# Gated mix of a state space layer and an MLP on one core: two spreading copies moved on VectorE, a group of TensorE transposes moved by one matmul and copied out in halves

## The chip, the cores and the metric

The kernel runs on one core of a Trainium2 chip. The metric is the device time of one execution in microseconds; the median of three executions is compared. The engines are called PE (TensorE matmul; PEld is its weight load), DVE (VectorE), ACT (ScalarE), POOL (GpSimd) and SP (SyncE, which only issues DMAs here).

## The reference, cut to what matters

```python
x = A_x                                              # 2048 rows of 448, bfloat16
g = sigmoid((x * gate_w).sum(-1, keepdims=True))
# a: Bu = x @ B_bar.T;  h[t] = Lam_bar * h[t-1] + Bu[t] (complex);  a = 2 Re(h @ C.T) + x * Dskip
# b: silu(x @ w1) @ w2                               # 448 -> 1792 -> 448
return g * a + (1 - g) * b
```

## The kernel before, in words

The 2048 rows of `x` are read as 1024 pairs, so that every pair has an even and an odd row of 448 columns. `XT` holds `x` transposed, with its columns on the 128 partitions: blocks 0 to 3 for the even rows, 4 to 7 for the odd ones. The 448 columns are three full blocks of 128 (`j` = 0, 1, 2) and a rest of 64 (`j` = 3). Block 3 is filled with the columns 384 to 511 of a pair, so the last 64 columns of the even row lie in its lower 64 partitions. `XR` holds that rest a second time in the other 64 partitions: matmuls of 64 rows can then run in both halves of the PE array at once. The rows are worked in four parts of 512: even 0, even 1, odd 0, odd 1.

There is no scheduler. A `Tracker` writes one list of instructions per engine in the order of the program text. Before each operation it adds the waits that the named buffers ask for: a reader waits for the last writer of a name, and a writer waits for the last writer and for all readers since then. Each of the eight PSUM banks is one such name (`ps0` to `ps7`), whatever part of the bank is used. Engines run their lists strictly in order.

**The front, up to about 10 us.** Part even 0 doesn't come by a transposing DMA. It is loaded as rows into `XH` (the start of `XN`) in six DMAs, `XA0` to `XA3` for the columns 0 to 255 and `XB0`, `XB1` for the columns 256 to 383 and 384 to 511. PE transposes 128x128 squares of it into PSUM (`turn_k`, line 493), and DVE copies them into `XT` (`turned_k` line 503 for one square, `turned_x` line 509 for two or four). `turn_x(j, i)` issues the two squares `2i` and `2i+1` of block `j`. All of them go to bank 6 for `j` = 0 and 2 and to bank 7 for `j` = 1 and 3 unless another is given.

`ffn1_first` is a generator that runs the first six column blocks of `x @ w1` for part even 0 in six banks, and stops at fixed places so that the transposes can be put between (line 435). For `j` = 0 its matmuls cover 128 or 256 columns; for `j` = 1 and 2 there are six matmuls each over all 512 columns, numbered `n` = 0 to 5. The order of PE's list in the front is: three matmuls of `j` = 1, four small matmuls that turn parameter rows into columns (`mm_cols`, line 474), four transposes for block 2, the other three matmuls of `j` = 1, four transposes for block 3, six matmuls of `j` = 2, and then three pairs with the rest (`ffn1_rem`, line 449). From there on `lanes` (line 362) carries the rest of `x @ w1` and of the state space input, and ACT applies silu (line 457).

**DVE's list from 10 to 27 us** prepares tables of sines and cosines. `phases(pt)` (lines 614 and 616) is two operations over 128x1024 float32, on POOL for `pt` = 0 and 3 and on DVE for 2 and 1; `phases2(pt)` (line 621) is a DVE operation with two inputs that needs the result of `phases(pt)`. In between lie: two copies that spread the rows `gate_w` and `Dskip` from 32 to 64 and from 64 to 128 partitions of `GD` (line 672, 896 bfloat16 a partition); `decays` (four operations on 128x4); `swap_xr("dve", 1, 0)` (line 241), which fills `XR` for the last columns of part even 1; and copies in `BT` and `BR` (lines 680 and 682). `GD` is read by `gate` (654) and `skip` (662), which come behind `phases2(1)`. Line 901 is the first step of the scan and reads what PE has put in PSUM; the first one follows the `XR` copies of the odd rows (line 238).

Of the kernel before, what the change touches and what calls it, by code (L numbers as in the profile page):

```python
# [150 lines left out]
def gated_mix(nc, A_x, A_Lambda_re, A_Lambda_im, A_B_re, A_B_im, A_C_re, A_C_im, A_log_dt,  # L151
              A_Dskip, B_x, B_w1, B_w2, gate_w, out):
    with ExitStack() as ctx:
# [75 lines left out]
            return T.dma("sp", lambda e: e.dma_start_transpose(dst, src), reads=reads,  # L229
                         writes=[key, *also], group=group)  # L230

        XE = [(["XTe000", "XTe001", "XTe010", "XTe011", "XTe02"], ["XTe03"]), (["XTe1"], ["XTer1"])]
        XO = [([f"XTo{h}"], [f"XTr{h}"]) for h in range(2)]

        def swap_xr(eng, h, odd):
            hs = slice(h * 512, (h + 1) * 512)
            if odd:
                T.op(eng, lambda e: e.tensor_copy(XR[0:64, hs], XT[64:128, 7, hs]), reads=XO[h][1],
                     writes=[f"XR{h}b"])
            else:  # L240
                T.op(eng, lambda e: e.tensor_copy(XR[64:128, hs], XT[0:64, 3, hs]), reads=XE[h][1],
                     writes=[f"XR{h}a"])
# [93 lines left out]
        def nxt():  # L336
            n_bank[0] += 1
            return BANKS[(n_bank[0] - 1) % len(BANKS)]
# [7 lines left out]
        def rem_keys(odd, h, p):  # L346
            return (XO if odd else XE)[h][1] if (p is UP) == bool(odd) else [f"XR{h}{'b' if odd else 'a'}"]

# [48 lines left out]
        def ff(fb):  # L397
            i, c = fb // 2, fb % 2
            return i + 3 * c if i < 3 else i + 3 + 2 * c if i < 5 else i + 5 + 2 * c

        def wj(fb):
            i, c = fb // 2, fb % 2
            return [f"W1Ej0{c}", "W1Ej1", "W1Ej2"] if i < 3 else ["W1Ed0", "W1Ed2"] if i < 5 else ["W1Ee0", "W1Ee1"]

        def w1(fb):
            return lambda p, j: W1E[p, j, ff(fb) * 128:(ff(fb) + 1) * 128] if j < 3 else \
                W1E[p, j, fb // 2 * 128:(fb // 2 + 1) * 128]

        def rem_ffn1(odd, h, fb):
            return [*[f"W1E{'r' if fb < 6 else 's'}{c}" for c in range(2)], *rem_keys(odd, h, LO), *rem_keys(odd, h, UP)]  # L410
# [6 lines left out]
        def ffn1_pair(c, fb, p=None):  # L417
            odd, h = c // 2, c % 2
            banks = at(p) if p is not None else [nxt(), nxt()]
            return (*[(banks[i], odd, h, w1(fb + i)) for i in range(2)],  # L420
                    wj(fb) + wj(fb + 1) + (XO if odd else XE)[h][0], rem_ffn1(odd, h, fb),
                    lambda: ffn1_act(c, fb, banks[0], 2))

        def ffn1_first():
            banks = [nxt() for _ in range(NF1)]
            for fb in (0, 2, 4):
                T.op("pe", lambda pe, fb=fb, bank=banks[fb]: pe.matmul(
                    ps[:, bank, 0:128], W1E[:, 0, ff(fb) * 128:(ff(fb) + 1) * 128], XT[:, 0, 0:128],
                    start=True, stop=True), reads=["W1Ej00", "XTe000a"], writes=[f"ps{banks[fb]}"])
            for j, h in ((0, 0), (0, 1), (1, None), (2, None)):  # L430
                for n, fb in enumerate((0, 2, 4, 1, 3, 5)):
                    k = h == 0 and n < 3
                    c = slice(0, 512) if h is None else slice(128 if k else 256 * h, 256 * h + 256)
                    bank = banks[fb]
                    T.op("pe", lambda pe, fb=fb, bank=bank, j=j, h=h, c=c, k=k: pe.matmul(  # L435
                        ps[:, bank, c], W1E[:, j, ff(fb) * 128:(ff(fb) + 1) * 128], XT[:, j, c],
                        start=(h == 0 and not k), stop=(h == 0 and not k), skip_group_check=(h != 0 or k)),
                        reads=[f"W1Ej{j}" if j else f"W1Ej0{fb % 2}"] + (
                            ["XTe02"] if j == 2 else [f"XTe0{j}{h}"] if h is not None else [f"XTe0{j}0", f"XTe0{j}1"]),
                        writes=[f"ps{bank}"])  # L440
                    if (j, h, n) in ((0, 0, 2), (0, 0, 5), (1, None, 2), (1, None, 5)):
                        yield
            yield banks

# [10 lines left out]
        def ffn1_act(c, fb, bank, n=1):  # L455
            a = AT[c % 2]
            T.op("act", lambda e: e.activation(a[:, fb:fb + n, :], ps[:, bank:bank + n, :], AF.Silu),  # L457
                 reads=[f"ps{bank + i}" for i in range(n)], writes=[f"AT{c % 2}_{fb + i}" for i in range(n)])

        def ffn1(c, f0=0, ahead=None):  # L460
            for fb in range(f0, NFB, 2):
                pair(*ffn1_pair(c, fb), last=(c == 3 and fb == NFB - 2))
                if ahead and fb == 8:
                    ahead()
                yield
# [31 lines left out]
        def turn_x(j, i):  # L497
            for k in (2 * i, 2 * i + 1):
                turn_k(j, k)
# [6 lines left out]
        def turned_x(j, i=None, b=None):  # L506
            c, key = (slice(0, 512), f"XTe0{j}") if i is None else (slice(256 * i, 256 * i + 256), f"XTe0{j}{i}")
            b = PB[j] if b is None else b
            T.op("dve", lambda e: e.tensor_copy(XT[:, j, c], ps[:, b, 0:256].bitcast(BF16)[:, c]),
                 reads=[f"ps{b}"], writes=[key])  # L510
# [5 lines left out]
        turned_x(1, 0)  # L516
        warm(1, 4)
        first = ffn1_first()
        next(first)
        for k in (2, 3):  # L520
# [3 lines left out]
        for k in (2, 3):  # L524
# [5 lines left out]
        T.op("dve", lambda e: e.tensor_copy(  # L530
            PV[:, :, :], ps[:, 7, 256:288].rearrange("p (t c) -> p t c", c=8)[:, :, 0:4]),
            reads=["pv", "ps7"], writes=["PV"])
        for i in range(2):
            turn_x(2, i)
        turned_x(2)
        next(first)
        for i in range(2):
            turn_x(3, i)
# [12 lines left out]
        def c1(n, pt):  # L551
            i = pc(n)
            return P[:, i, pt:pt + 1]
# [33 lines left out]
        first = next(first)  # L587
# [6 lines left out]
        def decays():  # L594
            ptt("lr", col("mag"), col("cs"), ALU.mult, ["mag", "cs"])
            ptt("li", col("mag"), col("sn"), ALU.mult, ["mag", "sn"])
            pts("nli", col("li"), -1.0, None, ALU.mult, ALU.bypass, ["li"])
            T.op("dve", lambda e: e.tensor_tensor(c1("lis", 3), c1("li", 3), SG[:, 0:1], ALU.mult),
                 reads=["li"] + SGN, writes=["lis"])
# [6 lines left out]
        def phase(pt):  # L606
            if pt < 3:
                return FP[:, pt, :]
            return Q3[:, :, :].rearrange("p a b -> p (a b)").bitcast(F32)

        def phases(pt, eng="pool"):
            f2 = "f2s" if pt == 3 else "f2"
            X, RR = phase(pt), G[:, GP[pt], :]
            T.op(eng, lambda e: e.tensor_scalar(X, IOTA[:, :], c1(f2, pt), 0.0, ALU.mult, ALU.add),
                 reads=["IOTA", f2], writes=[f"F{pt}"])
            T.op(eng, lambda e: e.tensor_scalar(RR, X, 1.0, MAGIC, ALU.mult, ALU.add),
                 reads=[f"F{pt}"], writes=[f"G{GP[pt]}"])

        def phases2(pt):
            X, RR = phase(pt), G[:, GP[pt], :]  # L620
            T.op("dve", lambda e: e.scalar_tensor_tensor(X, RR, MAGIC, X, ALU.subtract, ALU.subtract),
                 reads=[f"F{pt}", f"G{GP[pt]}"], writes=[f"F{pt}"])
# [45 lines left out]

        phases(0)
        phases(2, "dve")  # L670
        for n in (32, 64):
            T.op("dve", lambda e, n=n: e.tensor_copy(GD[n:2 * n, :, :], GD[0:n, :, :]), reads=["GW", "DB"],
                 writes=["GW", "DB"])
        phases2(0)
        decays()
        swap_xr("dve", 1, 0)
        phases2(2)
        phases(3)
        phases(1, "dve")
# [168 lines left out]
        def bt(p, j, m):  # L848
            if m == 6:
                return BR[p, j, :]  # L850
            c = (m // 2) * 128 + D * (m % 2)
            return BT[p, j, c:c + 128]
# [3 lines left out]
        def bu_even(pt, h, p=None, q=None):  # L856
# [4 lines left out]
            def done():  # L861
# [5 lines left out]

            return (*[(b[i], 0, h, lambda p, j, i=i: bt(p, j, m + i)) for i in range(2)], BTK[0:2] + XE[h][0],
                    BTK + XE[h][0] + rem_keys(0, h, LO) + rem_keys(0, h, UP), done)

# [5 lines left out]
        def bu3_even(p, q):  # L876
            b = at(p)

            def done():
# [7 lines left out]

            return (*[(b[h], 0, h, lambda p, j: bt(p, j, 6)) for h in range(2)], ["BR"] + XE[0][0] + XE[1][0],
                    ["BR"] + rem_keys(0, 0, LO) + rem_keys(0, 1, UP), done)
# [278 lines left out]
        f = ffn1(2)  # L1168
# [70 lines left out]
def bass_gated_mix__ssm_conv_s5__dense_activation_silu__prompt_kernel(nc, *args):  # L1239
    gated_mix(nc, *args)  # L1240
# [28 lines left out]
```

## Time and profile before

| | |
|---|---|
| median of 3 runs | 136.72 us (136.68 to 136.97) |
| the profiled execution | 136.32 us, its span 134.8 us, granted PE clock 1.0 |
| busy in the span | PE 131.4 us (97%), DVE 115.5 (86%), ACT 93.7 (70%), POOL 15.9 (12%) |
| chain that ended last | PE 93%, DMA 3%, ACT's queue 1%, DVE 1% |
| DMA | 11.78 MB, mean 87 GB/s |

The span runs from the first to the last instruction; the rest of the execution's time lies around it. In a timeline a line gives the start in us from the start of the span, the duration, the engine, the line of the kernel, the operation, and in brackets the idle time before it with what ended it. Matmuls are pipelined: a 128x512 matmul is recorded with 0.38 us, but in a dense stream one starts every 0.216 us, and a 128x128 transpose every 0.055 us. A few matmul records are missing from a trace.

### The profile page before, as it was taken

How to read it: one execution, taken by the hardware profiler on the slowest of the kernel's cores; microseconds unless marked ns; L12 is line 12 of the kernel's file. 1: busy time of each engine (PE TensorE's matmuls, PEld its weight loads, DVE VectorE, ACT ScalarE, POOL GpSimd, SP SyncE). 2: the span in 40 equal slices, each digit the busy share in tenths (PEclk: the TensorE clock that was granted, in tenths of full speed). 3: DMA queues.
4: the chain of work that ended last, by engine and by line, in shares of the span. 5: the costliest groups of instructions: out<-in, count | busy, mean ns of one | idle time of the engine just before them, and what ended most of it. 6: DMA issues, size and time to landing. Idle time of an engine off the chain costs nothing.

```text
span 134.8 us, 2637 instructions
## 1 busy us (share of the span) xinstructions
PE 131.4 (97%) x1074; PEld 65.7 (49%) x1075; DVE 115.5 (86%) x154; ACT 93.7 (70%) x146; POOL 15.9 (12%) x32
## 2 busy tenths in 40 slices
PE   7899999999999999999999999999999999999993
PEld 7544444444444554444445544445555555555552
DVE  1379999917999798999999999999999999994554
ACT  0469698899939999769999597796124337879200
POOL 7109358550000000000000000000000000000000
DMA  3999959996994310000211000000000000222123
GB/s 103 258 284 191 181 129 220 179 379 182 264 188 98 71 46 0 0 0 5 66 45 45 5 0 0 0 5 0 0 0 0 0 0 15 92 94 76 68 81 124
DMA packets 25248, 11.78 MB, mean 87 GB/s; under 512 B 17619, under 2 KB 24726, under 8 KB 25238
## 3 DMA queue, kind: packets, MB, share of 16 engines
q1 hardware_dynamic: 23252, 10.47, 33.4%
q10 hardware_dynamic: 1986, 1.17, 3.0%
q8 instruction: 8, 0.13, 0.4%
q14 instruction: 2, 0.02, 0.0%
HBM read 5.34 MB, written 1.84 MB: 53 GB/s over the span
## 4 chain that ended last, share of the span: by engine, by line
PE 93%; DMA 3%; ACTq 1%; DVE 1%; issue 0%
PE ps L362 44%; PE ps L801 16%; PE ps L816 16%; PE ps L1054 15%; DMA XN<-in_A_x_dram 3%; PE ps L435 1%; ACTq L226 1%; DVE TMPS L1078 1%; PE ps L449 1%; PE ps L493 0%
## 5 line engine op out<-in xcount | busy, mean ns | idle before, releaser
L362 PE MATMUL ps<-XT,W1E 64*128 64x512 bf16 x325 | 41.4, 376 | 0.0
L457 ACT ACTIVATE AT<-ps 128x1024 bf16<-128x1024 f32 x28 | 28.2, 1019 | 7.4 <-PE ps L362 7.2
L362 PEld LDWEIGHTS ps<-XT,W1E 64*128 64x128 bf16 x325 | 16.9, 94 | 19.0 <-ACT AT L457 0.3
L362 PE MATMUL ps<-XT,BT 64*128 64x512 bf16 x156 | 22.4, 377 | 0.0
L816 PE MATMUL ps<-W,AT 64*128 64x448 bf16 x224 | 21.5, 349 | 0.0
L801 PE MATMUL ps<-W,AT 128*128 128x448 bf16 x112 | 21.4, 353 | 0.0
L816 PEld LDWEIGHTS ps<-W,AT 64*128 64x128 bf16 x224 | 10.9, 94 | 10.4
L801 PEld LDWEIGHTS ps<-W,AT 128*128 128x128 bf16 x112 | 10.9, 98 | 10.5 <-issue 0.4
L845 ACT ACTIVATE BT<-ps,GT 128x448 bf16<-128x448 f32 x8 | 5.1, 633 | 13.2 <-PE ps L801 13.2
L901 DVE SCALAR_TENSOR_TENSOR HS<-VE,P,ps 128x512 bf16<-128x512 bf16 (+1 forms) x13 | 9.6, 780 | 3.8 <-PE ps L362 3.8
L362 PEld LDWEIGHTS ps<-XT,BT 64*128 64x128 bf16 x156 | 8.1, 94 | 9.3 <-DVE HS L901 0.4
L945 DVE TENSOR_TENSOR_SCAN G<-P,Q 128x1024 f32<-128x1024 f32 (+1 forms) x6 | 11.4, 1922 | 0.0
L1054 PE MATMUL ps<-CO,VE 128*128 128x448 bf16 (+2 forms) x63 | 11.1, 332 | 0.0
L1054 PE MATMUL ps<-CO,HS 128*128 128x448 bf16 x56 | 11.1, 353 | 0.0
L362 PE MATMUL ps<-XR,W1E 64*128 64x512 bf16 x25 | 9.3, 376 | 0.0
L1054 PEld LDWEIGHTS ps<-CO,VE 128*128 128x128 bf16 x63 | 6.0, 98 | 4.8
L1054 PEld LDWEIGHTS ps<-CO,HS 128*128 128x128 bf16 x56 | 5.5, 98 | 5.1
L898 DVE TENSOR_TENSOR Q<-G,COS 128x2048 bf16<-128x2048 f32 (+1 forms) x4 | 7.0, 1756 | 0.1
L898 DVE TENSOR_TENSOR Q<-G,SIN 128x2048 bf16<-128x2048 f32 (+1 forms) x4 | 7.0, 1751 | 0.0
L863 ACT ACTIVATE VE<-ps 128x1024 bf16<-128x1024 f32 x6 | 6.1, 1019 | 1.2 <-PE ps L362 1.2
L865 ACT ACTIVATE ps<-VE,P 128x1024 f32<-128x1024 bf16 x6 | 6.7, 1118 | 0.2
L901 DVE SCALAR_TENSOR_TENSOR VE<-HS,P,FP 128x512 bf16<-128x512 bf16 (+1 forms) x7 | 6.6, 977 | 0.1
(126 smaller groups left out, 181.2 us busy)
## 6 DMA issues: line engine op xcount, KB each, us to landing
W<-in_B_w_dram SPq DMA_DIRECT2D x2, 784.0 KB, 5.9
XN<-in_A_x_dram SPq DMA_DIRECT2D x1, 896.0 KB, 5.3
out_dram<-OT SPq DMA_DIRECT2D x8, 112.0 KB, 1.7
out_dram<-TMPS SPq DMA_DIRECT2D x7, 112.0 KB, 1.7
HS<-HS SPq DMA_DIRECT2D x4, 128.0 KB, 2.3
XN<-in_A_x_dram SPq DMA_DIRECT2D x1, 384.0 KB, 3.8
W1E<-in_B_w_dram SPq DMA_DIRECT2D x1, 256.0 KB, 5.0
W1E<-in_B_w_dram ACTq DMA_DIRECT2D x1, 256.0 KB, 5.3
```

Source lines behind the costliest of these rows:

```text
L226: return T.dma(eng, lambda e: e.dma_start(dst, src), writes=[key], group=group)
L362: ins = pe.matmul(ps[:, bank, :], w(p, j), xh(odd, h, j, p), start=start and j == js[0], stop=stop and j == js[-1], skip_group_check=seeded)
L457: T.op("act", lambda e: e.activation(a[:, fb:fb + n, :], ps[:, bank:bank + n, :], AF.Silu), reads=[f"ps{bank + i}" for i in range(n)], wri ...
L801: ins = pe.matmul(ps[:, bank, 0:D], a[:, fb, q * 128:(q + 1) * 128], W2[:, ff(fb), :], start=(first and fb == 0), stop=(fb == NFB - 1), sk ...
L816: ins = pe.matmul(ps[:, bank, 0:D], a[p, fb, q * 128:(q + 1) * 128], W2[p, ff(fb), :], start=(start and fb == 0), stop=(not start and fb = ...
L845: T.op("act", lambda e: e.activation(bs(tile), ps[:, bank, 0:D], AF.Copy, scale=sc), reads=[f"ps{bank}", "GT2" if h else "GRI"], writes=ks)
L863: T.op("act", lambda e: e.activation(VE[:, m:m + 2, hs], ps[:, b[0]:b[0] + 2, :], AF.Copy), reads=[f"ps{i}" for i in b], writes=vs)
L865: T.op("act", lambda e: e.activation(ps[:, o[0]:o[0] + 2, :], VE[:, m:m + 2, hs], AF.Copy, scale=c1("lr", pt)), reads=vs + ["lr"], writes= ...
L898: T.op("dve", lambda e: e.tensor_tensor(o, a, b, op), reads=reads, writes=writes)
L901: T.op("dve", lambda e: e.scalar_tensor_tensor(o, a, s, b, ALU.mult, ALU.add), reads=reads, writes=writes)
L945: T.op("dve", lambda e: e.tensor_tensor_scan(G[:, c, w], rb, Q1[:, c, w], init, ALU.mult, ALU.add), reads=[f"Q1{c}", "rr", f"G{c}"], write ...
L1054: ins = pe.matmul(ps[:, bank, c], state(kt, odd, m), CO[:, m, c], start=False, stop=(m == YB[-1]), skip_group_check=True)
```

## The change

Two independent edits, both in the order of the text.

1. The transposes of block 2 move behind one more matmul of `j` = 1 (`n` = 3), for which `ffn1_first` gets one more stop. The copy of the block out of bank 6 is made in two halves of 256 columns, each right behind the two transposes that it reads. The name `XTe02` becomes `XTe020` and `XTe021`, and every reader takes both.
2. The two spreading copies of `GD` move behind `phases2(0)` and `swap_xr("dve", 1, 0)` in DVE's list.

```diff
-        XE = [([..., "XTe02"], ["XTe03"]), (["XTe1"], ["XTer1"])]
+        XE = [([..., "XTe020", "XTe021"], ["XTe03"]), (["XTe1"], ["XTer1"])]
...
-                            ["XTe02"] if j == 2 else ...
+                            ["XTe020", "XTe021"] if j == 2 else ...
...
-                    if (j, h, n) in ((0, 0, 2), (0, 0, 5), (1, None, 2), (1, None, 5)):
+                    if (j, h, n) in ((0, 0, 2), (0, 0, 5), (1, None, 2), (1, None, 3), (1, None, 5)):
                         yield
...
+        next(first)
         for i in range(2):
             turn_x(2, i)
-        turned_x(2)
+            turned_x(2, i)
         next(first)
...
         phases(0)
         phases(2, "dve")
+        phases2(0)
+        swap_xr("dve", 1, 0)
         for n in (32, 64):
             T.op("dve", lambda e, n=n: e.tensor_copy(GD[n:2 * n, :, :], GD[0:n, :, :]), reads=["GW", "DB"],
                  writes=["GW", "DB"])
-        phases2(0)
         decays()
-        swap_xr("dve", 1, 0)
         phases2(2)
```

The order of PE's list in the front is then: three matmuls of `j` = 1, `mm_cols`, the matmul `n` = 3, two transposes, two transposes, two matmuls of `j` = 1, four transposes for block 3, six matmuls of `j` = 2.

More of the change, by code (lines that the diff above doesn't have):

```diff
@@ L230, in ldt @@
                          writes=[key, *also], group=group)
-        XE = [(["XTe000", "XTe001", "XTe010", "XTe011", "XTe02"], ["XTe03"]), (["XTe1"], ["XTer1"])]
+        XE = [(["XTe000", "XTe001", "XTe010", "XTe011", "XTe020", "XTe021"], ["XTe03"]), (["XTe1"], ["XTer1"])]
         XO = [([f"XTo{h}"], [f"XTr{h}"]) for h in range(2)]
@@ L438, in ffn1_first @@
                         reads=[f"W1Ej{j}" if j else f"W1Ej0{fb % 2}"] + (
-                            ["XTe02"] if j == 2 else [f"XTe0{j}{h}"] if h is not None else [f"XTe0{j}0", f"XTe0{j}1"]),
+                            ["XTe020", "XTe021"] if j == 2 else [f"XTe0{j}{h}"] if h is not None else [f"XTe0{j}0", f"XTe0{j}1"]),
                         writes=[f"ps{bank}"])
-                    if (j, h, n) in ((0, 0, 2), (0, 0, 5), (1, None, 2), (1, None, 5)):
+                    if (j, h, n) in ((0, 0, 2), (0, 0, 5), (1, None, 2), (1, None, 3), (1, None, 5)):
                         yield
```

## The prediction

> **What bounds the kernel now.** I read the chain that ended last first, since it says which engine a microsecond has to be taken from. It is the following, in order of time (start, duration, what):
>
> ```profile
> 2.77 4.00 DMA XN<-in_A_x_dram
> 6.77 0.05 issue
> 6.82 0.40 PE ps L493 x4
> 7.21 0.05 issue
> 7.27 0.59 PE ps L435 x2
> 7.86 0.22 PE ps L493 x4
> 8.08 1.29 PE ps L435 x6
> 9.38 0.75 PE ps L449 x6
> 10.13 31.76 PE ps L362 x294
> ```
>
> From 6.77 us, when the DMA with columns 256 to 383 (XB0) lands, the chain is PE without a hole. The matmul records bear that out: with 0.216 us for 512 columns, start to start, the steps from 7.05 us to the last matmul leave only two holes, 0.096 us before line 449 and 0.092 us before line 801, both where PE changes between matmuls of 128 and of 64 rows. So a time that the front of PE's list gains or loses arrives at the end unchanged; what DVE, ACT and POOL gain arrives only if PE waits for it.
>
> Second, the timeline of the front, for the place of edit 1, and two rows of 5 us, which show the same kind of hand-over:
>
> ```profile
> 4.89 0.22 DVE L503 COPY XT<-ps 128x128 bf16<-128x128 bf16 x1
> ...
> 5.02 0.11 PEld L493 LDWEIGHTS ps<-ID,XN 128*128 128x128 bf16 x2 [0.15 <-DVE XT L503]
> ...
> 5.35 0.29 DVE L509 COPY XT<-ps 128x256 bf16<-128x256 bf16 x1 [0.25 <-PE ps L493]
> ...
> 6.47 0.24 PE L474 MATMUL ps<-ID,R 128*128 128x4 bf16 x4
> ...
> 6.81 0.23 PEld L493 LDWEIGHTS ps<-ID,XN 128*128 128x128 bf16 x4 [0.19 <-DMA XN<-in_A_x_dram]
> 6.82 0.40 PE L493 MATMUL ps<-ID,XN 128*128 128x128 bf16 x4
> ...
> 7.25 0.42 DVE L509 COPY XT<-ps 128x512 bf16<-128x512 bf16 x1 [0.32 <-PE ps L493]
> ```
>
> PE has a hole of 0.24 us in front of the transposes (the last of mm_cols starts at 6.55 and takes a step of 0.025) and waits there for XB0. The copy of the block starts 0.258 us after the last transpose started (6.994 to 7.252), as at 5 us (5.092 to 5.350).
>
> Third, the timeline of DVE and POOL for edit 2, and from the list of waits the first long wait of DVE behind it:
>
> ```profile
> 12.00 1.37 POOL L616 TENSOR_SCALAR G<-FP 128x1024 f32<-128x1024 f32 x1
> ...
> 12.49 2.40 DVE L672 COPY GD<-GD 32x896 bf16<-32x896 bf16 x2
> ...
> 13.53 1.12 POOL L614 TENSOR_SCALAR Q<-IOTA,P 128x1024 f32<-128x1024 f32 x1 [0.17 <-POOL G L616]
> ...
> 14.93 1.23 DVE L621 SCALAR_TENSOR_TENSOR FP<-G,FP 128x1024 f32<-128x1024 f32 x1
> ```
>
> ```profile
> DVE HS L901 <- PE ps L362: 3.8, 2, 3.2
> ```
>
> **Edit 1, the matmul that moves (gain).** Matmul n = 3 has nothing to wait for behind mm_cols: its weights and block 1 are those of n = 0 to 2. It starts at about 6.58 and its 0.216 us step ends at 6.80, so it lies whole in the 0.24 us hole. XB0 lands at 6.771 and its weight load can start at 6.81 as now, so the transposes keep their place: gain 0.216 us.
>
> **Edit 1, the halves (loss).** All four transposes write bank 6. The first half copy now stands between the second and the third of them and reads that bank, so the third transpose must wait for it: a wait that the order of the changed kernel shows on PE (line 493, on DVE) and that before doesn't have. In PE's list everything is queued behind it. Its price from rows: the second transpose starts at 6.882 as now; 0.258 us later the half copy can start, at 7.140 (DVE is free, its PV copy ends at 6.93); 128x256 takes 0.292 us (the row at 5.35); from the end of a DVE copy to the waiting transpose are 0.057 us (4.970 to 5.027, and 5.102 to 5.158 in the next wait). The third transpose starts at 6.882 + 0.258 + 0.292 + 0.057 = 7.489. In the stream it would have been 0.055 us behind the second, so the hole is 0.552 us. Nothing can fill it, for PE runs in order.
>
> **Sum for PE.** The fourth transpose starts at 7.554 (the step behind a wait is 0.065, as from 6.817 to 6.882), n = 4 and 5 at 7.609 and 7.825, the transposes of block 3 from 8.041, the first matmul of j = 2 at 8.265. Before it starts at 7.921: 0.34 us later, which is 0.552 - 0.216 and a slow step.
>
> **Can something else be later still?** The second half copy starts 0.258 us behind the fourth transpose, at 7.81, and ends at 8.10; the first matmul of j = 2 needs 0.06 us from there, 8.16, and comes at 8.265. XB1 landed at 7.476 and the weights of j = 2 at 7.681. On DVE two operations for the decay rates (0.15 and 0.16 us) wait behind both halves: they start at 8.02 in place of 7.59, 0.43 later, and ACT's exponential, its table load (1.28 us) and the two row DMAs of GD in ACT's queue with them (they landed at 11.44 and 11.66, and GD is now touched only behind 14.9). ACT is then free for the first silu at 10.00, and that silu, which starts at 9.74 now, comes with PE at 10.09. So 0.08 us of cover is left; without it PE would lose the excess through the banks. The copies of block 3 and of XR shift by the same 0.34 as PE.
>
> [...] The rows give 0.292 us for a half and 0.425 for the whole, so two halves cost 0.159 us more. [...]
>
> **Edit 2.** No instruction is added. The two GD copies took 1.11 and 1.26 us, although a copy of 64x896 in BT takes 0.39 (line 680). They end 0.24 us after the POOL operations beside them end (13.604 after 13.363, 14.895 after 14.652): they stood waiting for POOL. Once moved, phases2(0) must itself wait for POOL's line 616, which ends at 13.36; the GD copies covered that wait, and DVE now stands idle from 12.46 to about 13.42, some 0.95 us. Whether the operation then goes ahead of POOL's next one (start 13.53) the trace doesn't show. If it does, it ends at 14.65, and the XR copy (0.32 with its gap), two GD copies (0.42 each) and decays (0.52) follow: phases2(2) starts at 16.33 to 17.3, with none or one 0.95 us POOL operation in the way. If POOL goes first, phases2(0) is held to 14.65 and phases2(2) starts at 17.53. Before it starts at 16.91: -0.6 to +0.6 us. I take +0.2, since POOL's next operation will most likely fall on the XR copy. POOL's own later phases move as much.
>
> The nearest row for the two operations meeting is a POOL operation on 128x4 that takes 0.34 us by itself and 1.01 when it starts at 22.41 beside a line 621 that runs to 23.37. [...]
>
> On PE all of this costs nothing, at either end: the next reader of DVE's work is the matmul at 17.96, which needs the XR copy that ended at 16.88 and now ends earlier; the BT copy is read 2.0 us after it ends, the odd XR copies 2.9 and 4.4 us after. What is left of a delay ends in DVE's idle 3.2 us before line 901 at 30.55, which waits for PE. Without that cover the 0.6 us would come on top.
>
> **Rivals.** *The half copy doesn't hold PE* (faster). Then only the 0.216 us count, giving 136.50. This happens if the third transpose starts less than 0.27 us (0.216 + 0.055) after the second. Against it: the one copy alone takes 0.292, and the hand-over at 5.02 us shows PE standing for just such a copy.
>
> *The weights are late anyway* (little or no change). The weights of the next pairs landed at 9.557 us, and PE first needed them at 9.76: 0.2 us of room. The unprofiled runs were 0.4 us longer than the profiled one; if that is loads that land late, PE waits there before the change too, and up to all of the 0.34 is swallowed: 136.72 to 136.95. Against it: the profile shows no such wait.
>
> *The hole is bigger* (slower). If XB0 lands before 6.55, there was no hole to fill and the whole 0.55 counts: 137.27. The same sign has a silu that ACT starts late, beyond its 0.08 us.
>
> **How the numbers follow.** The profiled execution would take 136.32 + 0.34 = 136.66. The median stands 0.40 above it; the hole is a wait inside the chip and doesn't depend on that, so 136.72 + 0.34 = 137.06, 0.25% more. 0.2% of 136.72 is 0.27 us, about what a measurement of this kernel can tell from no change. Chances: my forecast 0.66, late weights 0.14, bigger hole 0.11, no hold 0.09. For the range I take late weights in full at its lower end and the bigger hole at its upper, with 0.10 us for the scatter of a median (the three runs lie 0.04 below to 0.25 above theirs): 136.62 to 137.37. Only no hold lies outside. Slower by over 0.2%: the bigger hole and 0.51 of the forecast's 0.66 (its 0.34 lies only 0.07 over the bound), 0.62. Within 0.2%: the other 0.15 and late weights, 0.29. Faster: 0.09.
>
> **What would show it.** In the profile after: no wait for XB0 of 0.19 us before line 493, but a hole of about 0.55 us between the second and the third transpose of block 2, ended by DVE line 509; two copies of 128x256 at about 7.14 and 7.81; the first matmul of j = 2 at 8.27; the span near 135.2; GD copies of about 0.4 us each, and DVE idle before line 621 near 13 us. I am wrong if the third transpose follows the second at once, if PE shows a new hole behind 8.3 us, or if the first matmul of j = 2 starts before 8.1.

## The result, and the profile after

The changed kernel takes 137.08 us (median of 22 runs, 136.39 to 137.78), the kernel before 136.72 (22 runs, 135.98 to 137.58). The ratio is 1.0031 with a 95% interval of 1.0016 to 1.0047: 0.42 us more, between 0.22 and 0.64. Two later comparisons of 12 runs, on two different chips, gave 1.0049 for edit 1 alone and 1.0050 for the full change. In the latter, one of the 12 runs, at 139.12 us, counts as slow and is left out. The forecast was 137.06, slower.

The profiled execution of the changed kernel took 136.39 us, the shortest of the 22, and its span is 134.8 us, the same as before. That alone would read as no change. The chain that ended last, in order of time, shows where the time is (start, duration, what):

```profile
3.68 0.33 PE ps L427 x3
...
6.27 0.08 PE ps L474 x4
...
6.43 0.29 PE ps L493 x2
6.72 0.02 issue
6.74 0.30 DVE XT L509
7.04 0.05 issue
7.09 0.29 PE ps L493 x2
7.37 0.43 PE ps L435 x2
7.80 0.22 PE ps L493 x4
8.03 1.29 PE ps L435 x6
```

A DVE copy has come into the chain, between two and two transposes, where there was none; behind the last line shown it is PE without a hole again, as before: from the first matmul of line 449 to the end of the span are 125.52 us in both profiles. So what differs between the two lies in the front. And the chain now goes back to the first matmuls instead of to XB0: in this execution XB0 landed at 6.01 us (before: 6.77), and the first weights of line 427 at 3.62 (before: 3.97), so PE's work began 0.35 us earlier. Counted from there, the first matmul of j = 2 comes 4.202 us after the first of line 427 (3.663 to 7.865), and 3.908 us before (4.013 to 7.921): 0.29 us more, although the execution of before had a wait of 0.24 us for XB0 in this stretch and the changed one has none. The earlier start of 0.35 us hides it in the span.

The timeline of the front shows the hold itself, with PE's idle time before the third transpose and what ended it in brackets:

```profile
6.43 0.27 PE L493 MATMUL ps<-ID,XN 128*128 128x128 bf16 x2
...
6.74 0.29 DVE L509 COPY XT<-ps 128x256 bf16<-128x256 bf16 x1 [0.17 <-PE ps L493]
7.08 0.11 PEld L493 LDWEIGHTS ps<-ID,XN 128*128 128x128 bf16 x2 [0.56 <-DVE XT L509]
7.09 0.29 PE L493 MATMUL ps<-ID,XN 128*128 128x128 bf16 x2 [0.39 <-DVE XT L509]
```

By the single records the second transpose starts at 6.484 and the third at 7.088. Less the step of 0.055 that is a hole of 0.549 us.

Edit 2, in the timeline of DVE and POOL and in the list of waits between 10 and 33 us:

```profile
11.94 1.37 POOL L617 TENSOR_SCALAR G<-FP 128x1024 f32<-128x1024 f32 x1
...
13.34 1.23 DVE L622 SCALAR_TENSOR_TENSOR FP<-G,FP 128x1024 f32<-128x1024 f32 x1 [0.93 <-POOL G L617]
...
13.47 2.08 POOL L615 TENSOR_SCALAR Q<-IOTA,P 128x1024 f32<-128x1024 f32 x1 [0.17 <-POOL G L617]
...
14.59 1.11 DVE L241 COPY XR<-XT 64x512 bf16<-64x512 bf16 x1
...
15.73 0.80 DVE L675 COPY GD<-GD 32x896 bf16<-32x896 bf16 x2
...
16.99 1.22 DVE L622 SCALAR_TENSOR_TENSOR FP<-G,FP 128x1024 f32<-128x1024 f32 x1
```

```profile
DVE HS L902 <- ACT VE L882: 3.1, 1, 3.1
```

The GD copies take 0.38 and 0.39 us in place of 1.11 and 1.26. What they lost is paid by others: DVE stands idle for 0.93 us, POOL's line 615 takes 2.08 us in place of 1.12, and the XR copy 1.11 in place of 0.29. phases2(2) starts at 16.99, and DVE still has 3.1 us of idle time before line 902.

### The profile page after: what moved, and what is told of

Its sections match the earlier page's. It is cut to its first block, busy times and chain, and to the rows that moved or that the text cites. A ratio compares the mean times of both kernels' runs of the same rounds, so it can differ in the third digit from the quotient of the medians.

```text
span 134.8 us, 2637 instructions
## 1 busy us (share of the span) xinstructions
PE 131.4 (98%) x1074; PEld 65.3 (48%) x1075; DVE 115.0 (85%) x155; ACT 93.8 (70%) x146; POOL 16.9 (13%) x32
## 3 DMA queue, kind: packets, MB, share of 16 engines
q10 hardware_dynamic: 1986, 1.17, 3.1%
## 4 chain that ended last, share of the span: by engine, by line
PE 97%; DVE 1%; issue 0%
PE ps L362 44%; PE ps L802 16%; PE ps L817 16%; PE ps L1055 15%; PE ps L435 3%; PE ps L483 2%; PE ps L493 1%; DVE TMPS L1079 1%; PE ps L449 1%; PE ps L427 0%; DVE XT L509 0%; PE ps L474 0%
## 5 line engine op out<-in xcount | busy, mean ns | idle before, releaser
L817 PEld LDWEIGHTS ps<-W,AT 64*128 64x128 bf16 x224 | 10.9, 94 | 10.4
```

Of the source, the lines that this page charges most:

```text
L817: ins = pe.matmul(ps[:, bank, 0:D], a[p, fb, q * 128:(q + 1) * 128], W2[p, ff(fb), :], start=(start and fb == 0), stop=(not start and fb = ...
```

## The experiments

All times were compared with the kernel before on the same chip. The theory: the half copy holds PE through the name of bank 6, and nothing else of the change costs anything. The rivals: the moved GD copies cost it; the move of the transposes costs it; two copies in place of one cost it; a hole in the front is swallowed by later waits.

**Edit 1 alone** (the full change without the moved GD copies).

> Edit 1 alone, GD copies where they were. If the half copy's hold of PE is the cause: the whole change, a hole of 0.55 us between the second and third transpose of block 2, and 0.2 to 0.55 us over before, as the full change has. If the moved GD copies are the cause: no difference from before beyond the scatter, and no more than 0.1 us.

Measured: 1.0049 (1.0032 to 1.0066), 137.23 against 136.59 us. The hole is 0.549 us (6.983 to 7.587, less the step). The timeline of this kernel also shows a wait for XB0 in front of it, which the changed kernel's profile hadn't:

```profile
6.92 0.28 PE L493 MATMUL ps<-ID,XN 128*128 128x128 bf16 x2 [0.16 <-DMA XN<-in_A_x_dram]
...
7.24 0.29 DVE L509 COPY XT<-ps 128x256 bf16<-128x256 bf16 x1 [0.27 <-PE ps L493]
7.58 0.11 PEld L493 LDWEIGHTS ps<-ID,XN 128*128 128x128 bf16 x2 [0.56 <-DVE XT L509]
```

Edit 1 by itself is enough for the whole loss. The forecast of "0.2 to 0.55 us" was passed by the middle of the measurement, 0.67 us, but not by its interval, 0.44 to 0.90.

**Edit 2 alone.**

```diff
         phases(2, "dve")
+        phases2(0)
+        swap_xr("dve", 1, 0)
         for n in (32, 64):
             ...
-        phases2(0)
         decays()
-        swap_xr("dve", 1, 0)
```

> Edit 2 alone. If the hold is the cause: same as before within 0.1 us, no new hole on PE; DVE idle some 0.9 us before line 621 near 13.4 us, GD copies 0.39 us each in place of 1.1 and 1.3, phases2(2) within 0.2 us of where it was. If the moved GD copies are the cause: 0.2 to 0.55 us over before.

Measured: 1.0009 (0.9991 to 1.0026). PE has no hole inside the transposes of block 2. It does wait 0.12 us in front of those of block 3, for XB1, which landed at 8.05 in this execution (before: 7.48); nothing of edit 2 comes ahead of that. DVE does the same as in the full change:

```profile
13.79 1.23 DVE L621 SCALAR_TENSOR_TENSOR FP<-G,FP 128x1024 f32<-128x1024 f32 x1 [0.93 <-POOL G L616]
...
15.05 1.10 DVE L241 COPY XR<-XT 64x512 bf16<-64x512 bf16 x1
...
16.18 0.81 DVE L674 COPY GD<-GD 32x896 bf16<-32x896 bf16 x2
```

phases2(2) starts 0.12 us later than before when both are counted from the first matmul of line 449. So the moved GD copies cost nothing that can be measured; they also bring nothing.

**The move without the halves.**

```diff
+        next(first)                 # the matmul n = 3 first
         for i in range(2):
             turn_x(2, i)
         turned_x(2)                 # one copy, as before
```

> The matmul n = 3 moved, but one whole copy behind all four transposes, so no hold between them. If the hold is the cause: no hole inside the transposes; the first matmul of j = 2 now waits up to 0.1 us for the copy of 512 columns; 0.22 us under before where PE waited for XB0, up to 0.1 over where it did not, so between -0.2 and +0.1 us. If moving the transposes is what costs: 0.2 to 0.55 us over before, as the full change.

Measured: 1.0006 (0.9989 to 1.0023), 136.75 us. No hole inside the transposes, which are one group again:

```profile
7.36 0.39 PE L493 MATMUL ps<-ID,XN 128*128 128x128 bf16 x4
```

The first matmul of j = 2 comes 0.117 us late (8.348 in place of 8.231), 0.14 us after the copy of 512 columns has ended (7.78 + 0.42): that is the small wait that halves would avoid. Edit 1 alone, on the same chip, differs from this kernel only in the two half copies; its 12 runs are on average 0.47 us longer (95% interval 0.22 to 0.72). So it is the halves that cost the time, not the move.

**The halves in two banks.**

```diff
-        PB = (6, 7, 6, 7)
+        PB = (6, 7, 6, 6)
...
+        next(first)
         for i in range(2):
-            turn_x(2, i)
-        turned_x(2)
+            for k in (2 * i, 2 * i + 1):
+                turn_k(2, k, 6 + i)
+            turned_x(2, i, 6 + i)
```

> Edit 1 with the second half of block 2 in bank 7 (and block 3 in bank 6), so the third transpose need not wait for the half copy, only for the PV copy out of bank 7. If the hold by the shared bank name is the cause: the hole falls from 0.55 to under 0.1 us, and the time is 0 to 0.2 us under before. If the cost lies in two copies in place of one, or in the move: still 0.2 to 0.55 us over before.

Measured: 1.0014 (0.9993 to 1.0036), 136.71 us, where edit 1 alone on the same chip took 137.23. Both have the move and both half copies; only the bank of the second half, and that of block 3, differs. The difference of the medians is 0.52 us, that of the averages of 12 runs each 0.38 (0.06 to 0.71). Timeline:

```profile
7.42 0.17 DVE L530 COPY PV<-ps 128x16 f32<-128x16 f32 x1 [1.25 <-PE ps L474]
7.46 0.48 PE L493 MATMUL ps<-ID,XN 128*128 128x128 bf16 x4
...
7.77 0.50 DVE L509 COPY XT<-ps 128x256 bf16<-128x256 bf16 x2 [0.17 <-PE ps L493]
...
8.79 0.28 PE L493 MATMUL ps<-ID,XN 128*128 128x128 bf16 x2 [0.42 <-DMA XN<-in_A_x_dram]
```

The four transposes are one group again, with a hole of 0.082 us between the second and the third, which is the wait for the PV copy in bank 7 (it ends at 7.593; 0.056 behind it, 7.649). So it is the shared bank that costs, not the number of copies. The expected gain of up to 0.2 us over before was not seen. This profile (of an execution of 137.52 us) shows a wait of 0.58 us for XB1, which landed at 8.74: the last line.

**The halves without the move.**

```diff
         for i in range(2):
             turn_x(2, i)
-        turned_x(2)
+            turned_x(2, i)
```

> The two half copies without the move of n = 3: the hold without what may set off against it. By the hold: a hole of 0.55 us between the second and third transpose, and 0.55 us over before in every execution whose loads are not later still, so 0.4 to 0.6 us; if the move was worth 0.22 us in most executions, this is 0.22 us slower than edit 1 alone, if XB0 has mostly landed by then, it is the same. If the hold costs nothing: the same as before.

Measured: 1.0038 (1.0017 to 1.0058), 137.12 against 136.45 us. The hole is 0.550 us (6.953 to 7.558), behind a wait of 0.12 us for XB0. It is not slower than edit 1 alone (by the medians 0.67 us over before, edit 1 alone 0.64), nor than the full change on the same chip, 137.26: the move sets nothing visible off against the hold. The intervals are too wide to rule out a few tenths.

**Three holds in place of one.**

```diff
+        for k in range(4):
+            turn_k(2, k, 6)
+            turned_k(2, k, 6)
```

> Edit 1 with a copy behind each of the four transposes, so three holds in place of one. A hold is 0.258 from the transpose to the copy, some 0.22 for a copy of 128 columns (line 503), 0.057 back, less the step of 0.055: 0.48 us each, 1.45 together. By the hold: three holes of 0.48 us, and 1.1 to 1.5 us over before. If holes in the front are swallowed by later waits: the same 0.3 to 0.5 us as the full change.

Measured: 1.0115 (1.0086 to 1.0144) from 6 runs, between 1.17 and 1.96 us. The timeline has the pattern three times, 0.481, 0.494 and 0.496 us by the records, 1.47 in sum:

```profile
7.20 0.22 PE L493 MATMUL ps<-ID,XN 128*128 128x128 bf16 x1
...
7.45 0.23 DVE L503 COPY XT<-ps 128x128 bf16<-128x128 bf16 x1
...
7.74 0.23 PE L493 MATMUL ps<-ID,XN 128*128 128x128 bf16 x1 [0.32 <-DVE XT L503]
8.00 0.23 DVE L503 COPY XT<-ps 128x128 bf16<-128x128 bf16 x1 [0.32 <-PE ps L493]
8.28 0.10 PEld L493 LDWEIGHTS ps<-ID,XN 128*128 128x128 bf16 x1 [0.45 <-DVE XT L503]
```

The loss grows with the holds, so later waits don't swallow them. In this one profile PE also stands 0.43 us at 33.4, waiting for line 902, which began some 0.4 us late; what kept it the profile doesn't show. It may be why the middle, 1.57 us, lies above the sum of the holes.

**The full change again.**

> The full change again, beside the other runs on one chip: 0.3 to 0.55 us over before. If edit 2 gives something back, it stays below edit 1 alone (which stood 0.6 us over before) by more than the intervals.

Measured: 1.0050 (1.0028 to 1.0071), 137.26 (median of 11 runs) against 136.45 us; hole 0.551 us. Edit 2 gives nothing back: edit 1 alone, on another chip, stood at 1.0049. In this execution XB0 landed at 6.57, long before PE was ready for it, and the first transposes show no wait:

```profile
7.69 0.27 PE L493 MATMUL ps<-ID,XN 128*128 128x128 bf16 x2
...
8.35 0.29 PE L493 MATMUL ps<-ID,XN 128*128 128x128 bf16 x2 [0.39 <-DVE XT L509]
```

**XB0 made late, without and with the move.** Two kernels that size the move. In both XB0 is issued behind the weights of j = 2 in ACT's queue; the second also has n = 3 in front of the transposes and the halves in two banks.

```diff
-        for i, eng in enumerate(("act", "sp")):
-            ld(eng, XH[...256 + 128 * i...], ..., XA[4 + i])
-        ld_w("act", 2)
+        ld_xb(1, "sp")
+        ld_w("act", 2)
+        ld_xb(0, "act")
```

> The kernel before with XB0 issued one place later in ACT's queue, behind the weights of j = 2, so that PE waits for it in nearly every execution. This sizes the one term in which the predictions of the change differ from execution to execution. If PE waits for XB0 in front of block 2's transposes: a wait of 0.4 to 1.0 us there and the same over before. If XB0 lands early anyway: same as before.

> The same late XB0 with n = 3 moved in front of the transposes and the halves in two banks, so without the hold. If the move is worth its 0.216 us whenever PE waits for XB0 by as much: 0.1 to 0.22 us under the kernel with late XB0 alone, the matmul n = 3 inside the wait in the profile. If the move is worth nothing even then: the same as that kernel.

Measured: 1.0014 (0.9994 to 1.0035) and 1.0036 (1.0020 to 1.0053). In the profile of the first PE waits 0.67 us for XB0, which landed at 7.93; in that of the second it landed at 7.02, before PE was ready, and there was no wait. The pair is inconclusive: the wait was not there in every execution, and with the move the kernel was not faster. What the move is worth when PE does wait was seen in no measured time.

## Why the prediction was right

The mechanism is right: the half copy holds PE, and the hole has the predicted size. That the time fits to 0.02 us, 137.06 against 137.08, is luck. One term of the sum, the gain from the move, was too large; waits for XB1 are not in it at all; and the later comparisons, on other chips, put edit 1 alone and the full change 0.67 and 0.68 us over before, twice the forecast 0.34. By its steps:

**The hold.** Predicted 0.552 us from four rows of before; the five profiles with the half copies in one bank show 0.549, 0.549, 0.550, 0.551 and, with a shorter copy, 0.481 to 0.496 for a predicted 0.48. The parts are as predicted too: 0.256 us from transpose to copy (6.484 to 6.740), 0.292 for the copy, 0.056 back (7.032 to 7.088). Edit 1 in two banks, where the hole falls to 0.08 us and the loss from 0.67 to 0.19 (between -0.10 and 0.49), shows that the hold is the cause.

**The gain from the moved matmul.** This is the term that was mis-sized. 0.216 us was read from the one profile, in which PE waited 0.24 us for XB0. Of the nine profiles with XB0 at its place, three have such a wait: 0.24 before, 0.30 in edit 1 alone (with n = 3 in it), 0.12 in the halves without the move. PE was through with mm_cols at 6.58 to 6.77 us in these three, and XB0 landed at 6.77 to 6.87. In five others PE came later, at 6.98 to 7.48, and in that of after, where it came at 6.21, XB0 had landed at 6.01. Capped at 0.216 that is on average (0.216 + 0.216 + 0.119) / 9 = 0.06 us. Then the sum is 0.55 - 0.06 = 0.49 us, which lies in the intervals of all three comparisons with the hold and the move: 0.22 to 0.64 in the first, 0.44 to 0.90 for edit 1 alone, 0.38 to 0.97 for the repetition. The prediction had this case as the rival of the bigger hole, at 0.11; it is the more frequent one. That nine executions give the share of all of them is not shown.

**A term that is not in the sum.** Where XB1 lands late, PE waits for it in front of the transposes of block 3, and a hold just before would be covered by that wait. Of the four profiles without the hold (before, edit 2 alone, the whole copy, two banks) two show such a wait, 0.12 and 0.58 us. In such executions the change would cost that much less, down to nothing; no profile shows the hold and this wait together. Four profiles give no share, so how much of the hold is covered on average stays open; the measured losses, 0.42 to 0.68 us by their middles, leave room for little of it.

**What else could be late.** The two decay operations started at 7.62, 0.40 before the predicted 8.02, as the whole front was. One hand-over was taken too small: 0.06 us from the end of the second half copy to the first matmul of j = 2. With the whole copy, where this wait is exposed, it is 0.145 us (8.203 to 8.348). With that the predicted 8.16 becomes 8.25, against the 8.265 of the sum: the sum held with 0.02 us to spare. ACT's load ended at 9.60 and the first silu started at 9.69: the cover of 0.08 us held.

**Edit 2.** Predicted: idle DVE 0.95 us, phases2(0) ahead of POOL's next operation, that operation on the XR copy, GD copies of 0.4, phases2(2) 0.2 us later. Measured 0.93, that order, 0.38 and 0.39, and 0.13 later (16.99 against 16.91 less the 0.06 by which the front was early). POOL's line 615 starts 0.14 us behind DVE's line 622 and takes 0.96 us longer than before (2.08 against 1.12), and the XR copy behind line 622 takes 0.82 longer (1.11 against 0.29). One row was misread, without consequence: the 0.34 us of a POOL operation on 128x4 "by itself" (20.81 us) lie beside the DVE copy of line 682; with DVE idle such an operation takes 0.20 (from 27.48 us on). The cover (3.1 us before line 902) held, and the time of edit 2 alone is that of before.

**Rivals.** No hold is refuted by the hole. Late weights did not swallow it on average: the loss stood in every comparison. In single executions a late load may, as the waits for XB1 suggest. The bigger hole stands in six of the nine profiles.

**What would show it.** The hole, its end by DVE line 509, the two half copies, the short GD copies and the idle DVE came as named. The points in time did not: the half copies started at 6.74 and 7.41 in place of 7.14 and 7.81, the span near 135.2 was 134.8, and the first matmul of j = 2 started at 7.87, although "before 8.1" had been named as a sign of being wrong. That sign misled: it counted from the start of the span, and this execution's front ran 0.40 us ahead. I had taken the profiled execution of before as the measure for that of after, but single executions differ by as much as the change.

## What to carry to other kernels

Splitting a copy can let the reader start sooner only if the writer of the second part may go on. In this kernel dependencies are kept by bank: the next write into the bank waited for the copy, and PE, which was the bound, stood for the whole round trip (0.26 + 0.29 + 0.06 us). With the copies in two banks, the hole was 0.08 us in place of 0.55. Before a wait for a load is counted as room to be filled, look in more than one profile for it. And where two profiles are compared, count from an event that both have, not from the start of the span.

## What the runs showed of the hardware that was not expected

PE started at half its later pace and took that up at a time that differed from execution to execution. The step of a 128-column matmul fell from 0.107 to 0.055 us; the long steps ended at 4.3 us in the profile of before, at 3.4 in that of after, and as late as 6.2 in that of the repetition, although the first matmul always started near 0.8 us and the granted clock is given as 1.00 throughout. Between the earliest and the latest of these ends lie 2.8 us. Counted from the first matmul, the long steps lasted 2.6 to 5.4 us, with waits of PE in between. Together with the landing of the loads (XB0 at 6.0 to 6.9 us in the nine profiles, XB1 at 7.2 to 8.7) this goes with a front of varying length: the first matmul of line 449 starts at 8.7 to 10.4 us in the nine profiles, the holds taken off. What follows it takes 125.5 us in all of them but the one with three holds (125.9). So the scatter between these executions comes from the front, and it is about as wide as that of the kernel before in all its runs, 135.97 to 137.60 us.
